# Decay terms and mask rows of three pairs as columns: the first batch of an attention and MLP kernel, recast

## The chip, the core and the metric

The kernel runs on one core of one Trainium2 chip. The metric is the device time of one launch in microseconds (us). A core has five engines that take their instructions in order, each from its own queue: PE (TensorE, matrix products), DVE (VectorE), ACT (ScalarE), POOL (GpSimd) and SP (SyncE, which here only issues DMAs). PEld is PE's loading of weights. Matmul results land in PSUM, which has eight banks for 512 f32 columns each; everything else lies in SBUF, with 128 partitions.

## The reference

Attention for 8 batches of 8 heads, 576 positions, 64 columns a head, with a decay that grows along the sequence, and then an MLP with a hard-swish gate:

```python
scores = scale * np.matmul(q, k.transpose(0, 1, 3, 2))
cum = np.cumsum(np.maximum(s, 0.0), axis=-1)
bias = -(cum[:, :, :, None] - cum[:, :, None, :])
scores = np.where(causal, -1000000000.0, scores + np.minimum(bias, 0.0))
attn = softmax(scores)                      # over the last axis
x = (attn @ v)                              # heads side by side: 4608 x 512
h = x @ w_in                                # 512 -> 2048
out = (h * np.clip(h + 3.0, 0.0, 6.0) / 6.0) @ w_out   # 2048 -> 512
```

## The kernel before

**Pairs.** The 64 heads are worked off as 32 pairs; a pair is two heads of one batch, so 1152 rows of q and of k. Three slots (`p % 3`) hold the transposed operands `qT` and `kT`, the values `v_h`, and three more the exponentials `Pm`. A score is one matmul over 128 partitions: rows 0 to 63 are the head's columns, and the other 64 rows carry the decay (three f16 parts of the running sum on the side of k, one on the side of q, each against ones) and a coarse causal mask of 60 rows. What the coarse mask leaves is cut by POOL (`affine_select`, L295).

**A pair's steps.** `load_qk` and `load_v` (L136 to L157) issue the loads on SP, in pieces of 64 f32 values. `cast_qk` (L167) makes f16 on POOL, `transpose_group` (L242) transposes q and k together on PE, five and four tiles, and DVE copies the halves to `qT` and `kT` (L253). `load_aug` (L159) brings the four decay rows from a scratch in DRAM, which the kernel has filled at its start (L469, L472). The mask rows of the three slots are written once (`mask_rows`, L125). For slot 0 the decay rows come straight from SBUF by eight small DMAs (L463 to L468). `scores_bank` (L272) makes four PSUM banks of scores a head, and ACT the exponentials (L290). `attend` (L320) sums with v (L331), and after a pair's second head DVE normalises (L341, L343). `x_transpose` (L356) puts the result into `xT`, by PE for the first eight pairs (L369, L377).

From pair 10 on the operands come another way: POOL builds `xb`, rows of 64 columns of q or k with the 64 decay and mask columns beside them (`cast_columns`, from `dec` and `xaug`), and one DMA transposes the whole.

**The layers.** Blocks of 512 tokens. `m1(n, f)` (L408) is four matmuls into a bank, then ACT (L416) and DVE (L417) make the gated f16 value in `gT`. `m2(n, t4, part)` (L430) is four of the sixteen matmuls of an output tile, and after the fourth part DVE scales it (L439) and SP stores it (L441). Weights come by POOL's queue with a cast (L383, L390).

**The order.** It is written by hand. Pairs 0 to 3 and the scores of pair 4 stand alone; then `weave` deals the tasks of four pairs among the MLP tasks of one block or more, by the costs beside each task. The MLP of block n can begin when the batch that it reads is in `xT`. At the start `keep_warm` gives PE idle work (L450).

PSUM: three banks with tag S (scores, transposes later on), two for O, two with tag M (`bank`: layers, early transposes, `keep_warm`), one with tag Y (outputs).

Of the kernel before, what the change touches and what calls it, by code (L numbers as in the profile page):

```python
# [9 lines left out]
F32 = mybir.dt.float32  # L10
# [6 lines left out]
def kernel(  # L17
# [29 lines left out]
    NS = 3  # L47

# [3 lines left out]

    def bank():
        return psum.tile([128, 512], F32, tag="M", bufs=2, name="bank")

    ident_dram = nc.inline_tensor(np.eye(128, dtype=np.float16), name="ident_f16")

    gran = np.arange(SEQ) // GRAN
    rows = np.arange(60)
    amask_np = np.ones((2, 64, SEQ), dtype=np.float16)  # L60
    amask_np[0, 4:64] = gran[None, :] == rows[:, None]
    amask_np[1, 4:64] = np.where(gran[None, :] < rows[:, None], -16384.0, 0.0)
    amask_dram = nc.inline_tensor(amask_np, name="amask")

    row = np.arange(W2).reshape(NTR, 128).T % SEQ
    xaug_np = np.concatenate([amask_np[1][:, row], amask_np[0][:, row]], axis=2)
    xaug_dram = nc.inline_tensor(
        np.ascontiguousarray(xaug_np.transpose(1, 2, 0)).reshape(128, 2 * NTR * 64),
        name="xaug",
    )  # L70
# [14 lines left out]
    xb = cpool.tile([128, 2, 2 * NTR, 128], F16, tag="c_xb")  # L85
# [9 lines left out]
    amask = work.tile([128, 2, SEQ], F16, tag="amask", bufs=1)  # L95
    s_sb = work.tile([NH, SEQ], F32, tag="s0", bufs=1)
    nc.sync.dma_start(out=s_sb, in_=s.rearrange("b h t -> (b h) t"))
    nc.scalar.dma_start(out=amask[64:128], in_=amask_dram.ap().rearrange("i p t -> p i t"))
# [20 lines left out]
    nc.gpsimd.memset(warm, 0.0)  # L119
    nc.gpsimd.memset(kT[:, :, W2:W2 + 64], 0.0)  # L120
    nc.gpsimd.memset(v_f[64:128, :, :, 4, :], 0.0)
    nc.gpsimd.memset(v_h[:, :, :, :, D:VW], 1.0)
    nc.gpsimd.memset(Pm[:, :, 1600:PW], 1.0)

    def mask_rows(sl, copy):  # L125
        for i, dst in enumerate((kT, qT)):
            copy(
                out=dst[64:128, sl, 0:W2].rearrange("p (h t) -> p h t", h=2),
                in_=amask[64:128, i:i + 1, :].to_broadcast([64, 2, SEQ]),
            )  # L130
# [5 lines left out]
    def load_qk(p, eng):  # L136
        b, h0 = (2 * p) // H, (2 * p) % H
        t = work.tile([128, NTR, 2, D], F32, tag="qkf", bufs=3, name=f"qkf{p}")
        for i, src in enumerate((q, k)):
            rows = src[b, h0:h0 + 2].rearrange("h s d -> (h s) d")  # L140
            eng.dma_start(  # L141
                out=t[:, :, i, :], in_=rows.rearrange("(t p) d -> p t d", p=128)
            )
        qk_f[p] = t

    def load_v(p, eng):
        b, h0 = (2 * p) // H, (2 * p) % H
        sl = p % NS
        for hh in range(2):
            eng.dma_start(  # L150
                out=v_f[:, sl, hh, 0:4, :],
                in_=v[b, h0 + hh, 0:512].rearrange("(t p) d -> p t d", p=128),
            )
        eng.dma_start(
            out=v_f[0:64, sl, :, 4, :],
            in_=v[b, h0:h0 + 2, 512:SEQ].rearrange("h p d -> p h d"),
        )  # L157

    def load_aug(p, eng):  # L159
        sl = p % NS  # L160
        c0 = p * W2
        eng.dma_start(out=kT[64:67, sl, 0:W2], in_=kaug_dram[:, c0:c0 + W2])
        eng.dma_start(out=qT[67:68, sl, 0:W2], in_=qaug_dram[:, c0:c0 + W2])
# [6 lines left out]
    xaug = cpool.tile([128, 2 * NTR, 64], F16, tag="c_xaug")  # L170

    def load_columns():
        nc.sync.dma_start(out=xaug.rearrange("p t c -> p (t c)"), in_=xaug_dram.ap())

    def copy_columns():
        for i in range(2):
            nc.vector.tensor_copy(out=xb[:, i, :, 64:128], in_=xaug)

# [32 lines left out]
    def cast_columns(p):  # L211
# [5 lines left out]
        nc.gpsimd.tensor_copy(out=x[:, 0:NTR, D + 3:D + 4], in_=dec[:, :, 3:4, p])  # L217
# [8 lines left out]
    def cast_v(p):  # L226
        sl = p % NS
        copy = nc.vector.tensor_copy if p in (1, 2, 3, 4) else nc.gpsimd.tensor_copy
        copy(out=v_h[:, sl, :, :, 0:D], in_=v_f[:, sl])  # L229

    def half_bank(early):

        if early:
            return psum.tile([128, 640], F16, tag="M", bufs=2, name="pTm")
# [7 lines left out]
    def transpose_group(p, g):  # L242
        t0, t1 = ((0, 5), (5, 9))[g]
        n = (t1 - t0) * 128
        pT = half_bank(p < 5)
# [10 lines left out]


# [4 lines left out]
        (896, [(1, 256, 576), (4, 512, 576)]),  # L262
        (1280, [(2, 256, 576)]),
# [5 lines left out]
        (4, 4): 1216, (2, 2): 1280, (2, 3): 1408, (2, 4): 1536,  # L269
    }  # L270

    def scores_bank(hd, bi):  # L272
# [39 lines left out]
        elif bi == 2:  # L312
            mask(P[:, 1216:1280], [[1, 64]])
        else:
            mask(P[:, 1280:1408], [[1, 128]])
# [4 lines left out]
    def attend(hd):  # L320
# [17 lines left out]
        if hh == 1:  # L338
            Ov = O_tiles.pop(p)[:, :, 0:5 * VW].rearrange("p h (t e) -> p h t e", t=5)
            r = work.tile([128, 2, 5, 1], F32, tag="r")  # L340
            nc.vector.reciprocal(out=r, in_=Ov[:, :, :, D:D + 1])  # L341
            xs = work.tile([128, 5, 2, D], F16, tag="xs", name=f"xs{p}")
            nc.vector.tensor_tensor(  # L343
                out=xs.rearrange("p t h d -> p h t d"),
                in0=Ov[:, :, :, 0:D],
                in1=r.to_broadcast([128, 2, 5, D]),
                op=ALU.mult,
            )
            x_tiles[p] = xs
# [6 lines left out]
    def x_transpose(p):  # L356
# [10 lines left out]
        pX = half_bank(p < 3)  # L367
# [9 lines left out]
        nc.vector.tensor_copy(out=xT[:, hp, b * SEQ:(b + 1) * SEQ], in_=pX[:, 0:SEQ])  # L377
# [25 lines left out]
    def m1(n, f):  # L403
        if f == 0:
            gT[n] = work.tile([128, NF, 512], F16, tag="gT", bufs=2, name=f"gT{n}")
        ph = bank()
        for kc in range(KC):
# [6 lines left out]
            )  # L414
        trl = work.tile([128, 512], F32, tag="trl", bufs=3)
# [5 lines left out]
    def m2(n, t4, part):  # L421
# [15 lines left out]
        if part == 3:  # L437
# [3 lines left out]
            nc.sync.dma_start(out=out[r0:r0 + 128, :], in_=osb)  # L441
# [5 lines left out]
    def keep_warm(n):  # L447
        pw = bank()
# [4 lines left out]


    load_qk(0, nc.sync)
    load_v(0, nc.sync)
    load_qk(1, nc.sync)
    mask_rows(0, nc.scalar.copy)

    nc.scalar.activation(out=qaug, in_=c8, func=AF.Copy, scale=-1.0)  # L460
    for hh in range(2):
        c0, c1 = hh * SEQ, (hh + 1) * SEQ
        nc.sync.dma_start(out=kT[64:65, 0, c0:c1], in_=kaug[hh:hh + 1, 0, :])  # L463
        nc.scalar.dma_start(out=qT[67:68, 0, c0:c1], in_=qaug[hh:hh + 1, :])
    for hh in range(2):
        c0, c1 = hh * SEQ, (hh + 1) * SEQ
        nc.sync.dma_start(out=kT[65:66, 0, c0:c1], in_=kaug[hh:hh + 1, 1, :])
        nc.scalar.dma_start(out=kT[66:67, 0, c0:c1], in_=kaug[hh:hh + 1, 2, :])  # L468
    nc.sync.dma_start(  # L469
        out=kaug_dram.rearrange("r (h t) -> h r t", h=NH), in_=kaug  # L470
    )
    nc.sync.dma_start(out=qaug_dram.rearrange("r (h t) -> h (r t)", h=NH), in_=qaug)  # L472
    mask_rows(1, nc.scalar.copy)
    load_v(1, nc.sync)
    load_aug(1, nc.sync)
    load_qk(2, nc.sync)
    load_v(2, nc.sync)

    weights_at = {1: [(load_w_in, 0)], 2: [(load_w_in, 1)]}
    pairs_at = {0: [3], 1: [4], 2: [], 3: [5], 4: [6], 5: [7, 8]}  # L480

    def att_tasks(p):


        more = p + 1 < NP

        def loads():
            if p + 2 < PTD:
                load_aug(p + 2, nc.sync)
            if p == 5:  # L490
                load_columns()
            for m in pairs_at.get(p, [p + 3] if p + 3 < NP else []):
                load_qk(m, nc.sync)
                load_v(m, nc.sync)
            if 4 < p < PTD - 1:
                cast_qk(p + 1)

        def casts():
            if more:
                cast_v(p + 1)  # L500
            if p + 2 <= 4:
                cast_qk(p + 2)
# [3 lines left out]
            for load, c in weights_at.get(p, []):  # L506
                load(c)

        def scores(hd):
            return [(lambda bi=bi: scores_bank(hd, bi), 400) for bi in range(4)]  # L510

        tr = [[], []]
        if p + 1 < min(NP, PTD):
            tr = [[(lambda: transpose_group(p + 1, 0), 640)],
                  [(lambda: transpose_group(p + 1, 1), 512)]]
        here = tr if p != 4 else [[], []]
        late = [(lambda: attend(2 * p - 1), 1200)] if p > 0 else []
        back = [(lambda: x_transpose(p - 1), 0 if by_dma(p - 1) else 640)] if p > 0 else []
        a = [(loads, 0)]
        if p <= PXD:  # L520
            a += scores(2 * p) + here[0] + late
            a += scores(2 * p + 1) + [(casts, 0)] + here[1] + back
        else:
            s0, s1 = scores(2 * p), scores(2 * p + 1)
            a = late + (back + a if by_dma(p - 1) else a + s0[:2] + back)
            a += (s0 if by_dma(p - 1) else s0[2:]) + here[0]
            a += s1 + [(casts, 0)] + here[1]
        if p == 6:
            a += [(decay_columns, 640)]
        if p == 7:  # L530
            a += [(copy_columns, 0)]
        c = [(lambda: attend(2 * p), 1200)]
        if p == 4:
            c += [(lambda: cast_qk(p + 1), 0)] + tr[0] + tr[1]
        return a, c

    att_of = [[]]
    for p in range(NP):
        a, c = att_tasks(p)
        att_of[-1] += a  # L540
        if p % 4 == 0 and p > 0:
            att_of.append([])
        att_of[-1] += c
    att_of[-1] += [(lambda: attend(NH - 1), 1200), (lambda: x_transpose(NP - 1), 640)]
# [39 lines left out]
    keep_warm(18)  # L584
    cast_qk(0)
    transpose_group(0, 0)
    transpose_group(0, 1)
    mask_rows(2, nc.vector.tensor_copy)
# [53 lines left out]
```

## Time and profile before

| | us |
|---|---|
| time, median of 3 runs (lowest, highest) | 382.07 (380.73, 382.93) |
| span of the profiled run | 378.1 |
| PE busy | 353.6 |
| ACT busy | 210.4 |
| DVE busy | 190.8 |
| POOL busy | 146.4 |

Busy times are sums over the span. PE is busy for 94% of it, but matmuls are pipelined and their ends are modelled, so a busy PE may still run at half clock or below its rate. The share of DMA is the mean over the 16 DMA engines of the time that their packets took; it can pass 1 where packets overlap. Of 184621 packets, 177828 are under 512 bytes.

What a stage is limited by is not seen in these sums. It is read from three views: the busy times in stretches of the span, the chain of work that ended last (followed back from the end, each step to what released it), and the timeline, in which an arrow in brackets tells how long an engine was idle before an instruction and what ended that.

### The profile page before, as it was taken

To read this page: it belongs to the slowest core of one execution; us is meant where nothing else is said; L and a number is where in the kernel's file an instruction comes from. 1 tells how busy PE (TensorE), PEld (TensorE's weight loads), DVE (VectorE), ACT (ScalarE), POOL (GpSimd) and SP (SyncE) were. 2 spreads that over 40 slices of the span, in tenths; PEclk is the share of its full clock that TensorE was granted. 3 is DMA by queue.
4 is the path that set the end of the run, shared out by engine and by line. 5 is a ranking of instruction groups with operands and counts; after the bars stand their busy time and mean duration, and the time that the engine had idled before them with its cause. 6 is when DMAs were issued, how large, how long until landed. Compare 5 with 4: busy or idle time off the path is not lost.

```text
span 378.1 us, 7609 instructions
## 1 busy us (share of the span) xinstructions
PE 353.6 (94%) x2780; PEld 219.8 (58%) x2780; DVE 190.8 (50%) x329; ACT 210.4 (56%) x406; POOL 146.4 (39%) x375
## 2 busy tenths in 40 slices
PE   7766778899999999999999999999999999999995
PEld 3454455566666666666666666666666655555542
DVE  5554466875545444544444445445444554454531
ACT  4745466456866666666656666666666543443310
POOL 4365444364565444444444554454453100000000
PEclk9989699999999999999999999999999999999999
DMA  8699999945999999999999998999854001010011
GB/s 181 137 204 193 194 208 249 210 105 132 200 186 243 204 211 200 216 203 203 197 190 199 214 208 179 206 211 200 185 114 106 31 30 55 28 55 29 28 66 74
DMA packets 184621, 59.38 MB, mean 157 GB/s; under 512 B 177828, under 2 KB 178212, under 8 KB 184584
## 3 DMA queue, kind: packets, MB, share of 16 engines
q1 hardware_dynamic: 182536, 54.52, 68.2%
q0 software_dynamic: 1632, 4.19, 5.9%
q8 instruction: 22, 0.36, 0.4%
q10 hardware_dynamic: 416, 0.19, 0.2%
q14 instruction: 15, 0.12, 0.1%
HBM read 37.41 MB, written 9.73 MB: 125 GB/s over the span
## 4 chain that ended last, share of the span: by engine, by line
PE 82%; DMA 9%; DVE 3%; ACT 2%; SPq 1%; issue 1%; POOL 1%; POOLq 0%; ACTq 0%; DVEq 0%
PE bank L408 31%; PE po L430 30%; PE S L282 9%; PE O L331 7%; DMA qkf<-in_k_dram 5%; DMA v_f<-in_v_dram 3%; PE bank L430 3%; ACT Pm L290 2%; PE pT L369 1%; DMA s_sb<-in_s_dram 1%; PE bank L450 1%; SPq L141 1%; POOL t L167 1%; DVE qkT L253 1%; DVE kaug L115 0%
## 5 line engine op out<-in xcount | busy, mean ns | idle before, releaser
L416 ACT ACTIVATE trl<-bank,bias 128x512 f32<-128x512 f32 x144 | 99.5, 691 | 111.8 <-PE bank L408 110.8
L417 DVE SCALAR_TENSOR_TENSOR gT<-trl,bank 128x512 f16<-128x512 f32 x144 | 99.1, 688 | 121.8 <-ACT trl L416 121.8
L408 PE MATMUL bank<-xT,w_in 128*128 128x512 f16 x576 | 148.3, 383 | 1.3 <-DVE gT L417 1.3
L290 ACT ACTIVATE Pm<-S 128x384 f16<-128x384 f32 (+2 forms) x256 | 116.2, 505 | 32.3 <-PE S L282 30.6
L295 POOL TENSOR_SCALAR_AFFINE_SELECT Pm<-Pm 128x128 f16<-128x128 f16 (+2 forms) x256 | 79.0, 311 | 135.4 <-ACT Pm L290 126.6
L430 PE MATMUL po<-w_out_sb,gT 128*128 128x512 f16 x528 | 130.9, 379 | 0.0
L408 PEld LDWEIGHTS <-w_in 128*128 128x128 f16 x576 | 77.5, 146 | 31.6 <-issue 2.8
L430 PEld LDWEIGHTS <-gT 128*128 128x128 f16 x576 | 53.2, 98 | 51.4
L282 PE MATMUL S<-qkT 128*128 128x320 f16 (+4 forms) x448 | 70.2, 265 | 6.9 <-DVE qkT L253 2.3
L282 PEld LDWEIGHTS <-qkT 128*128 128x128 f16 x448 | 41.4, 99 | 34.2 <-DVE qkT L253 2.7
L331 PEld LDWEIGHTS <-Pm 128*128 128x128 f16 x960 | 39.1, 98 | 12.1 <-POOL Pm L295 0.4
L331 PE MATMUL O<-v_h,Pm 128*128 128x65 f16 x960 | 41.6, 195 | 0.3 <-POOL Pm L295 0.3
L343 DVE TENSOR_TENSOR xs<-O,r 128x640 f16<-128x640 f32 x32 | 26.4, 824 | 1.1
L213 POOL CAST xb<-qkf 128x1152 f16<-128x1152 f32 x22 | 25.3, 1149 | 0.0
L439 DVE TENSOR_SCALAR osb<-po 128x512 f32<-128x512 f32 x33 | 22.6, 685 | 5.0 <-PE po L430 5.0
L229 POOL CAST v_h<-v_f 128x640 f16<-128x640 f32 x28 | 20.6, 737 | 2.2 <-DMA v_f<-in_v_dram 2.2
L341 DVE RECIPROCAL r<-O 128x10 f32<-128x10 f32 x32 | 7.1, 220 | 25.6 <-PE O L331 25.4
L167 POOL CAST t<-qkf 128x1152 f16<-128x1152 f32 x10 | 11.8, 1177 | 12.2 <-DMA qkf<-in_k_dram 12.2
L238 PEld LDWEIGHTS <-t 128*128 128x128 f16 x90 | 6.3, 99 | 12.1 <-POOL t L167 8.2
L253 DVE COPY qkT<-pTm 64x640 f16<-64x640 f16 (+1 forms) x20 | 9.1, 453 | 7.8 <-PE pTm L238 7.6
L450 PE MATMUL bank<-warm 128*128 128x512 f16 x30 | 9.5, 487 | 2.2 <-POOL warm L119 1.4
L430 PE MATMUL bank<-w_out_sb,gT 128*128 128x512 f16 x48 | 11.3, 379 | 0.0
(40 smaller groups left out, 80.2 us busy)
## 6 DMA issues: line engine op xcount, KB each, us to landing
qkf<-in_q_dram SPq DMA_DIRECT2D x32, 288.0 KB, 3.6
qkf<-in_k_dram SPq DMA_DIRECT2D x32, 288.0 KB, 4.2
out_dram<-osb SPq DMA_DIRECT2D x36, 256.0 KB, 2.0
v_f<-in_v_dram SPq DMA_DIRECT2D x64, 128.0 KB, 3.6
w_in<-in_moe_w_in_dram POOLq DMA_DIRECT2D x2, 1024.0 KB, 11.0
w_out_sb<-in_moe_w_out_dram POOLq DMA_DIRECT2D x4, 512.0 KB, 8.3
v_f<-in_v_dram SPq DMA_DIRECT2D x32, 32.0 KB, 8.2
qkT<-xb SPq DMA_TRANSPOSE x22, 5.2
```

Of the source, the lines that this page charges most:

```text
L213: nc.gpsimd.tensor_copy(out=x.rearrange("p (i t) c -> p t i c", i=2)[:, :, :, 0:D], in_=qk_f.pop(p))
L229: copy(out=v_h[:, sl, :, :, 0:D], in_=v_f[:, sl])
L282: nc.tensor.matmul(out=S[:, c:c + hi - lo], lhsT=kT[:, sl, off + 128 * kt:off + 128 * (kt + 1)], rhs=qT[:, sl, off + lo:off + hi], start=( ...
L290: nc.scalar.activation(out=P[:, p0:p0 + n], in_=S[:, 0:n], func=AF.Exp, scale=0.125, bias=0.0)
L295: nc.gpsimd.affine_select(out=view, in_=view, pattern=pattern, compare_op=ALU.is_ge, fill=0.0, base=0, channel_multiplier=-1,)
L331: nc.tensor.matmul(out=O[:, hh, qt * VW:qt * VW + D + 1], lhsT=P[:, c:c + 128], rhs=v_h[:, sl, hh, kt, 0:D + 1], start=(qt == 0), stop=(qt ...
L343: nc.vector.tensor_tensor(out=xs.rearrange("p t h d -> p h t d"), in0=Ov[:, :, :, 0:D], in1=r.to_broadcast([128, 2, 5, D]), op=ALU.mult,)
L408: nc.tensor.matmul(out=ph, lhsT=w_in_t[f // 8][:, kc, f % 8, :], rhs=xT[:, kc, n * 512:(n + 1) * 512], start=(kc == 0), stop=(kc == KC - 1),)
L416: nc.scalar.activation(out=trl, in_=ph, func=AF.Relu, bias=bias3[:, 0:1], scale=1.0)
L417: nc.vector.scalar_tensor_tensor(out=gT[n][:, f, :], in0=trl, scalar=6.0, in1=ph, op0=ALU.min, op1=ALU.mult)
L430: nc.tensor.matmul(out=po, lhsT=gT[n][:, f, t4 * 128:(t4 + 1) * 128], rhs=w_out_sb[:, f, :], start=(f == 0), stop=(f == NF - 1),)
L439: nc.vector.tensor_scalar_mul(out=osb, in0=po, scalar1=1.0 / 6.0)
```

## The change

For pairs 0 to 2 the operands are now built as they already are from pair 10 on: q and k are each loaded with nine whole rows to a partition (2304 bytes in one piece), cast into `xb` (now three buffers) beside the 60 mask columns, which one DMA and a copy bring, and the four decay columns. These come from small matmuls of the decay rows with a part of the identity (`decay_first`, 27 matmuls of 64x6). A transpose of the whole 128 columns then gives operand, decay and mask together. As nine rows lie in a partition, the copies out of PSUM read with a step (`rows_of_head`). Mask rows in all slots are left by these transposes, and the decay row on the side of q moves from row 67 to 127.

For pairs 0 and 1, v is loaded by POOL's queue with the cast in the DMA. The early transposes have two PSUM banks of their own (tag T), which are given to `bank` when the layers begin. The loads of later pairs are issued right after the cast that frees their buffer (`own`), with `load_aug` of a pair apart from them. Outputs of block 0 are stored by ACT's queue in place of SP's. Block 0's first layer is no longer dealt among pairs 4 to 8 but mostly within pair 4, with the Y bank as a third bank; 12 instead of 8 parts of its second layer stand in the tasks of pairs 5 to 8, and 4 in the next block. The bank of scores (4, 4) moves from the third to the fourth bank of a head, so that a head has three masks in place of four. In the last pair of the first batch each head is normalised by itself.

```diff
+    ROWS = 3
-    xb = cpool.tile([128, 2, 2 * NTR, 128], F16, tag="c_xb")
+    xb = cpool.tile([128, 3, 2 * NTR, 128], F16, tag="c_xb")
...
+            if p < ROWS:
+                qk_f[p] = t.rearrange("p (i t d) -> p t i d", i=2, t=NTR)
+                eng.dma_start(
+                    out=t[:, i * NTR * D:(i + 1) * NTR * D],
+                    in_=rows.rearrange("(p t) d -> p (t d)", t=NTR),
+                )
...
+    load_v(0, nc.gpsimd)
+    load_v(1, nc.gpsimd)
...
+    def transpose_rows(p, i):
...
+        for t in range(NTR):
+            transpose_tile(
+                T_tiles[p, i][:, t * 128:(t + 1) * 128],
+                xb[:, p, NTR * i + t, :],
...
+    def rows_of_head(p, i, hh):
+        nc.vector.tensor_copy(
+            out=(qT, kT)[i][:, p, hh * SEQ:(hh + 1) * SEQ].rearrange("d (j t) -> d j t", t=NTR),
+            in_=T_tiles[p, i][:, 0:W2].rearrange("d (t j) -> d j t", j=128)[
+                :, hh * 64:(hh + 1) * 64
+            ],
+        )
...
+    def decay_first(pD, i, first, last):
+        src = kaug[:, i, :].rearrange("h (j t) -> h t j", t=NTR)
+        for t in range(NTR):
+            nc.tensor.matmul(
+                out=pD[0:64, t, :],
+                lhsT=src[:, t],
+                rhs=ident[0:NH, 0:2 * ROWS],
...
-        (896, [(1, 256, 576), (4, 512, 576)]),
-        (1280, [(2, 256, 576)]),
+        (896, [(1, 256, 576)]),
+        (1216, [(2, 256, 576), (4, 512, 576)]),
...
+            if n == 0 and f % 3 == 2:
+                phs[f] = psum.tile([128, 512], F32, tag="Y", name="ph")
...
+            eng = nc.scalar if n == 0 else nc.sync
+            eng.dma_start(out=out[r0:r0 + 128, :], in_=osb)
...
+    for p in range(3):
+        load_qk(p, nc.sync, columns9_dram if p == 0 else None)
     load_v(2, nc.sync)
+    cast_first(0, nc.scalar.copy, 0, 1)
+    copy_columns(0, nc.scalar.copy)
+    load_qk(3, nc.sync)
+    load_v(3, nc.sync)
...
+    def own(p):
+        cast_qk(p)
+        cast_v(p)
+        load(p + 3)
...
+    keep_warm(10)
+    decay_first(pD0, 0, True, True)
+    keep_warm(3)
+    decay_first(pD1[:, 0], 1, True, False)
...
+    transpose_rows(0, 0)
+    decay_first(pD1[:, 1], 2, False, True)
...
+    nc.gpsimd.tensor_copy(out=hold, in_=kaug[:, 2, SEQ - 1:SEQ])
+    nc.gpsimd.tensor_scalar_mul(out=qaug, in0=kaug[:, 0, :], scalar1=-1.0)
+    cast_first(1, nc.gpsimd.tensor_copy)
...
+    layers_begin()
+    x_transpose(2)
+    for f in range(2):
+        m1(0, f, range(3))
+    attend(7)
...
+    own(4)
+    weave(pair_behind_weights(4), m1_tasks(0)[3:], 0.95)
...
+    weave(att_of[1], m2_0[4:12])
+    weave(att_of[2], merged(m1_tasks(1), m2_0[12:], 1))
```

## The prediction

> **What bounds the kernel now.** I read the slices of the page first, since a mean over 378 us hides the stages:
>
> ```profile
> PE   7766778899999999999999999999999999999995
> PEclk9989699999999999999999999999999999999999
> DMA  8699999945999999999999998999854001010011
> ```
>
> TensorE is full from slice 10 (about 95 us) to the end. Only before that is there time to win, and there the DMA row is full. The table by stages (columns: stretch, length, busy PE, PEld, DVE, ACT, POOL, granted clock, DMA share, GB/s) gives sizes:
>
> ```profile
> 12.00:24.00 12.00, 7.53 (x77) 5.48 (x76) 4.76 (x11) 6.20 (x15) 4.92 (x14) 0.86 0.90 186
> 24.00:36.00 12.00, 8.42 (x141) 6.75 (x139) 7.37 (x17) 7.80 (x19) 9.59 (x24) 1.00 1.02 194
> 36.00:48.00 12.00, 8.60 (x50) 5.34 (x51) 4.58 (x10) 5.49 (x11) 4.99 (x12) 0.72 1.00 198
> 48.00:60.00 12.00, 10.04 (x95) 7.00 (x94) 8.39 (x16) 7.87 (x15) 4.67 (x11) 1.00 1.11 231
> 60.00:72.00 12.00, 9.10 (x91) 6.30 (x89) 8.48 (x16) 7.14 (x15) 6.07 (x13) 1.00 1.03 219
> 84.00:96.00 12.00, 12.00 (x127) 8.13 (x125) 7.10 (x14) 7.78 (x18) 5.81 (x16) 1.00 0.59 131
> ```
>
> From 12 to 72 us TensorE is idle 16.3 us, no other engine is full, and the DMA share stays near 1. The chain that ended last says which transfers:
>
> ```profile
> 15.93 3.96 DMA qkf<-in_k_dram
> 27.48 11.71 DMA v_f<-in_v_dram
> 49.85 13.93 DMA qkf<-in_k_dram
> ```
>
> The timeline shows the holes on TensorE that they leave (start, duration, what; in brackets the idle time before it):
>
> ```profile
> 12.59 0.27 PE L282 MATMUL S<-qkT 128*128 128x256 f16 x1
> 21.24 0.29 PE L238 MATMUL pTm<-ident,t 128*128 128x128 f16 x1 [3.41 <-POOL t L167]
> 36.64 0.28 PE L282 MATMUL S<-qkT 128*128 128x256 f16 x1 [2.12 <-DMA qkT<-kaug_scratch]
> 40.63 1.56 PE L282 MATMUL S<-qkT 128*128 128x256 f16 x7 [1.76 <-DVE qkT L253]
> 42.78 0.63 PE L408 MATMUL bank<-xT,w_in 128*128 128x512 f16 x1
> ```
>
> First scores start at 12.59, the first layer matmul at 42.78: 30.2 us for four pairs. Between 24.4 and 33.9, where no transfer was late, two pairs took 9.4 us, so four would take 19; some 11 us are waits for data, a clock of one half behind them included (0.86 and 0.72 above).
>
> **What the Trainium skill says.** "DMA: Bandwidth & Descriptors", section "Why small descriptors are slow (HBM only)", gives a 256-byte descriptor 27% overhead. The trace agrees and goes further: its records have 21 ns for a packet of 256 bytes and 114 ns for one of 2304 (0.082 against 0.049 ns a byte). The same page, "Issuing engines are not separate DMA queues": a queue more saves issue time and no bandwidth. No run here isolates that; I give the v loads on GpSimd's queue no bandwidth gain. "VectorE: DVE Perf Modes", section "Mode 2×_1P", wants neighbouring 16-bit elements for two a cycle; the new copies read PSUM with a step of 128. The trace agrees with the fast case: 64x640 f16 from PSUM in 0.488 us, 128x512 f32 in 0.685. "TensorE: Matmul & The Clock Gate", section "What's actually happening", gives half clock after some 3.4 us of idleness; the stretch of 0.5 behind the 3.41 us hole agrees.
>
> **The start (to first scores).** Removed: four mask copies on ACT (4 x 1.146) and two on DVE (2 x 0.872), the eight row DMAs of decay terms into slot 0 and the loads of such rows for pairs 1 and 2 (one held TensorE 0.6 us, L163), and two casts of v (1.25 on POOL, 0.49 on DVE). Added: 27 small matmuls (as L192: 10 in 0.65 us, so 0.6 us per nine), 4 + 2 small copies on ACT and 2 on DVE (0.18 to 0.28 each as L205), 18 transposes of q and k apart instead of 9 joint (0.8 per nine), four copies of 128x576. Those have no row. Below: 0.46, as the contiguous xT copy; above: 0.75, the f32 row plus 64 elements at one a cycle (0.685 + 0.067). I take 0.75, because of the step.
> In order: kaug row 0 at 6.1 us (as now), its nine matmuls 6.8, ACT's copies 7.4; row 1 at 7.4 and its matmuls 8.0; q transposed 8.8. Row 2 ends at about 8.2, as POOL now waits behind "hold" and the subtraction can cost 0.75 (as L113) instead of 1.58; if the collision stays, 9.0. Its matmuls come behind q's transposes, 9.4; decay copies 9.9; k transposed 10.6; one copy, 11.4. So first scores at 11.4 (11.0 to 13.0): **-1.2 us**. Behind "hold" on POOL stand qaug and pair 1's cast (0.7 and 1.15), done by 11.5 and needed at 12. Pair 0's data come in six issues at 0.6 each, k by 6 to 7; the v loads on POOL cost it 6 x 0.55 to 0.9 before 9 us, and attend(0) needs them only near 16.
>
> **The first four pairs.** Pairs 1 and 2 are now bound by DVE with the one T tile: per half, nine transposes (0.8), two copies (1.5), in turn, as T must be read before it is refilled. First scores of pair 1: 12.85 (pair 0's last copy) + 1.5 + 0.8 + 1.5 = 16.7. Pair 2: + columns 0.93 + 0.8 + 1.5 + normalisation 1.04 (0.22 + 0.82) + 1.5 = 22.5. Pair 3: transposed jointly, two halves (4 copies, 1.82) behind xT 0.46 and waits of 1.6 for scores: 26.4. Then one pair as today, 4.7, ends at 31.1; I put the first layer matmul at **31.5** (29.5 to 34). ACT hides below: 8 heads x 1.69 = 13.5 us; so does POOL: 8 x 1.12 of masks (one of four selects gone; two blocks in one 0.41) and some 6 us of casts. DMA: q,k rows of three pairs 3 x 1.8, v 4 x 1.3, columns and s 1.5, pair 3's q,k 2.6, so about 15 us: landed near 18. The wait of pair 3's load for ACT's cast of pair 0 (8.7 us) holds only SP's next loads, which are not needed before 23. So here **-10.1** more.
>
> **From there to the second block of layers.** Now: 42.78 to 88.70 (m1(1,0)), with 9 of m2's 16 parts of block 0 done; after: 13 parts, so compare with 88.70 + 4 x 0.864 = 92.15 (a group of four takes 0.864 in the chain). After, by TensorE: m1 0 to 2, attend(7), two x transposes: 4.0 (the last waits for ACT's copy, ~0.5), 35.5. Thirteen m1 groups 11.2 + pair 4 (2.8) + halves 0.8 + 0.5 of stalls: 50.8. The third bank removes today's 0.64 waits of L408 for DVE; the banks opened in T's place wait for its last readers, DVE's copies of pair 3, done by 26. Four parts of m2, decay columns 1.8, halves: 57. Then 9 parts 7.8 and 3.75 pairs at 2.8 (15.5 - 7.8 for 2.75 pairs between 73.2 and 88.7 now) + 0.5 of stalls for each pair: 20.2, so 77.2. Stores of block 0 stand on ACT: each waits for DVE's osb (0.69) with exponentials behind; I charge their part of those stalls. Gain 92.15 - 77.2 = **15.0** at this point.
>
> **Paying DMA.** From 77.2, 21 groups + attention as now (11.3) = 29.4, so block 2 would begin at 106.6 against 121.56. The packets do not shrink so much: shares times lengths up to 121.5 sum to 111.5 us of all 16 engines; minus 3 x 1.2 for rows, 107.9 must fit into 104.6 us. The share over 140 to 260 is 0.99, over 108 to 120 it was 1.19: 0 to 4.4 us late; I take 3.0. Behind that TensorE is full in both kernels (9.3 us a pair), so nothing is given back. Masks, stores of later blocks and transposes by DMA stay. Sum **-12.0** against the profiled span of 378.1, so 366.1; the shown runs lie higher (median 382.07, 380.73 to 382.93), and 12 less is **370.0**.
>
> **The rivals.**
> A, as summed (0.55): 366 to 374.
> B, DMA stays the bound (0.28): rows save only 3.6 us; v loads with cast send the same number of pieces, and the weights now start at 16 us among the loads. Then only idle DMA (share 0.05 at 10 to 12, 0.45 to 0.83 at 42 to 46: ~3 us) and the rows count: 3.6 + 3 = about 7, 375 (374 to 378). For it: shares over 1 for 50 us. Against it: they drop to 0.58 at 72 to 96 while TensorE works off stock, so demand there can move.
> C, slower (0.07): pairs 5 to 8 starve. A load of pair p+3 now goes out after POOL's cast of pair p, behind 4 issues of w_out, and m1 is already spent on pair 4, so nothing fills TensorE. Leads are 18 us (pair 8: 51 to 70) and 14 (pair 9). With landings as today (14) nothing is lost; it decides above the lead: were weights and loads to stretch them to 22, four pairs would each wait 4 to 5 us: 12 - 17, some 5 slower, 387.
> D, copies at 0.46 and no DMA debt (0.10): 3.5 + 3.0 more, 363.5 (362 to 366).
> The change may also fail its name: in the built order stores of block 1 on still stand ahead of loads on SP; only block 0's left it. So that part is worth nothing beyond the waits of L141 and L150 counted.
>
> **Numbers.** A and D lie wholly below, B too: faster 0.90; within 0.5% (1.9 us, about what a measurement of this kernel can tell from no change) 0.03, between B and C; slower 0.07. Range 364.5 to 377.5: it holds A, most of B and part of D, and leaves out C.
>
> **What would show it.** Right: first S matmul at 11 to 13; 128x576 copies near 0.75; first w_in matmul at 30 to 34; no TensorE wait over 1 us for DMA between 12 and 60; m1(1,0) near 77, block 2 near 110; clock 1.00 from 12. Wrong: holes on TensorE in 55 to 75 released by casts of qkf or v_f (C); a DMA share near 1 with PE holes at 80 to 110 (B); scores later than 14 (the chain through ACT and PSUM is longer than priced).

## The result, and the profile after

The changed kernel takes 386.05 us (median of 4 runs, 385.73 to 387.33), the kernel before 381.88 beside it (380.73 to 382.93). The ratio is 1.0116 with a 95% interval of 1.0079 to 1.0154: slower, by over twice the half per cent that the prediction took for no change. The forecast was 370.0 and faster. The profiled spans are 384.0 and 378.1 us. In all ratios of this document executions over 1.5 per cent above the fastest of the same kernel are left out.

The slices of the page after, to be laid beside those of before:

```profile
PE   7978798867999999999999999999999999999995
PEclk9699999898999999999999999999999999999999
DMA  8998999465799999999997989899954101001012
```

The thin place on TensorE has moved. Before, it lay ahead of 57 us (digits of 6 and 7); now most of these are better, and the two slices from 77 to 96 us are worse, 6 and 7 where 9 stood. The DMA row falls there to 6 and 5, so it isn't full where TensorE idles. The same stretches as before, from the table of busy times:

```profile
12.00:24.00 12.00, 10.20 (x111) 7.12 (x111) 7.92 (x14) 7.98 (x18) 5.78 (x13) 0.85 1.02 189
24.00:36.00 12.00, 9.31 (x133) 6.87 (x132) 7.76 (x17) 7.16 (x17) 8.14 (x19) 1.00 0.89 169
36.00:48.00 12.00, 9.34 (x68) 6.16 (x67) 7.32 (x14) 6.79 (x12) 3.28 (x6) 1.00 1.09 207
48.00:60.00 12.00, 11.74 (x111) 7.57 (x109) 8.62 (x22) 7.34 (x15) 3.53 (x7) 1.00 0.99 205
60.00:72.00 12.00, 9.46 (x68) 5.38 (x67) 5.63 (x16) 3.68 (x10) 3.94 (x8) 0.86 0.64 154
84.00:96.00 12.00, 8.09 (x80) 5.27 (x81) 6.66 (x14) 3.38 (x8) 7.37 (x13) 0.92 0.43 98
```

From 12 to 60 us TensorE is busier in every row than before. In the last two rows ACT is busy for less than a third of the time (3.68 and 3.38 us of 12), and TensorE idles beside it: the engines wait for each other. The chain that ended last holds no transfer between 10 and 60 us any more, where it held 3.96, 11.71 and 13.93 us of them. The timeline of TensorE says where the time went instead:

```profile
15.70 0.68 PE L365 MATMUL S<-qkT 128*128 128x256 f16 x5
...
34.31 0.60 PE L507 MATMUL bank<-xT,w_in 128*128 128x512 f16 x2
...
65.01 0.33 PE L365 MATMUL S<-qkT 128*128 128x320 f16 x2 [1.23 <-ACT Pm L373]
...
71.16 0.56 PE L365 MATMUL S<-qkT 128*128 128x256 f16 x4 [0.78 <-DVE qkT L284]
...
85.40 0.45 PE L269 MATMUL pT<-ident,t 128*128 128x128 f16 x5 [1.57 <-POOL t L194]
...
92.59 0.33 PE L365 MATMUL S<-qkT 128*128 128x320 f16 x2 [1.90 <-ACT Pm L373]
```

First scores come 3.1 us later than before, the first layer matmul 8.5 us earlier. From 57 to 96 us the holes are released by exponentials (L373), by POOL's cast of the next pair (L194) and by DVE's copies (L284), never by a transfer. The first matmul of the second block, m1(1,0), stands at 95.90 (before 88.70), that of the third, m1(2,0), at 127.91 (before 121.56). At m1(2,0) both kernels have done the same: 182 matmuls of scores, 390 of the products with v, 128 and 72 of the two layers. From there to the end of the span it is 256.5 us before and 256.1 after. So the whole difference arises before m1(2,0). Up to that point TensorE is idle 20.0 us before and 19.8 after: the 7.2 us of holes taken out between first scores and first layer matmul are given back, most of them between 57 and 96. TensorE's busy time grew from 101.5 to 108.1 us, and the stretches at half clock from 10.2 to 13.7.

### The profile page after: what moved, and what is told of

It reads as the page before. It is cut to its first block, busy times and chain, and to the rows that moved or that the text cites. A ratio compares the mean times of both kernels' runs of the same rounds, so it can differ in the third digit from the quotient of the medians.

```text
span 384.0 us, 7564 instructions
## 1 busy us (share of the span) xinstructions
PE 360.0 (94%) x2822; PEld 223.9 (58%) x2822; DVE 190.2 (50%) x328; ACT 210.4 (55%) x412; POOL 142.9 (37%) x322
## 4 chain that ended last, share of the span: by engine, by line
PE 79%; DVE 7%; ACT 5%; issue 3%; POOL 3%; DMA 3%; ACTq 0%; POOLq 0%
PE bank L507 29%; PE po L531 28%; PE S L365 9%; PE O L416 6%; ACT Pm L373 4%; PE bank L531 2%; DVE qkT L284 2%; DMA qkT<-xb 2%; PE pT L269 2%; POOL Pm L378 1%; PE pD L318 1%; POOL t L194 1%; DMA s_sb<-in_s_dram 1%; PE pT L459 1%; DVE qkT L307 1%
## 5 line engine op out<-in xcount | busy, mean ns | idle before, releaser
L518 DVE SCALAR_TENSOR_TENSOR gT<-trl,bank 128x512 f16<-128x512 f32 x139 | 95.4, 687 | 119.8 <-ACT trl L517 119.7
L517 ACT ACTIVATE trl<-bank,bias 128x512 f32<-128x512 f32 x139 | 95.9, 691 | 105.2 <-PE bank L507 103.3
L507 PE MATMUL bank<-xT,w_in 128*128 128x512 f16 x556 | 143.2, 383 | 3.0 <-DVE gT L518 1.8
L373 ACT ACTIVATE Pm<-S 128x384 f16<-128x384 f32 (+2 forms) x256 | 115.7, 507 | 39.2 <-PE S L365 27.9
L378 POOL TENSOR_SCALAR_AFFINE_SELECT Pm<-Pm 128x256 f16<-128x256 f16 (+1 forms) x192 | 70.4, 370 | 158.0 <-ACT Pm L373 154.0
L431 DVE TENSOR_TENSOR xs<-O,r 128x640 f16<-128x640 f32 (+1 forms) x33 | 26.5, 804 | 1.3 <-DVE r L430 0.2
L430 DVE RECIPROCAL r<-O 128x10 f32<-128x10 f32 (+1 forms) x33 | 7.2, 217 | 30.6 <-PE O L416 30.5
L284 DVE COPY qkT<-pT 64x640 f16<-64x640 f16 (+1 forms) x24 | 10.9, 454 | 11.4 <-PE pT L269 10.9
L307 DVE COPY qkT<-pT 128x576 f16<-128x576 f16 x10 | 7.2, 751 | 4.3 <-PE pT L269 4.3
L269 PE MATMUL pT<-ident,t 128*128 128x128 f16 x63 | 5.5, 229 | 3.4 <-POOL t L194 2.1
L553 PE MATMUL pw<-warm 128*128 128x512 f16 x18 | 7.4, 567 | 1.4 <-POOL warm L203 1.4
```

The lines of the kernel that those rows point to most:

```text
L373: nc.scalar.activation(out=P[:, p0:p0 + n], in_=S[:, 0:n], func=AF.Exp, scale=0.125, bias=0.0)
L378: nc.gpsimd.affine_select(out=view, in_=view, pattern=pattern, compare_op=ALU.is_ge, fill=0.0, base=0, channel_multiplier=-1,)
L431: nc.vector.tensor_tensor(out=x_tiles[p].rearrange("p t h d -> p h t d")[:, h0:hh + 1], in0=Ov[:, :, :, 0:D], in1=r.to_broadcast([128, hh ...
L507: nc.tensor.matmul(out=ph, lhsT=w_in_t[f // 8][:, kc, f % 8, :], rhs=xT[:, kc, n * 512:(n + 1) * 512], start=(kc == 0), stop=(kc == KC - 1),)
L517: nc.scalar.activation(out=trl, in_=ph, func=AF.Relu, bias=bias3[:, 0:1], scale=1.0)
L518: nc.vector.scalar_tensor_tensor(out=gT[n][:, f, :], in0=trl, scalar=6.0, in1=ph, op0=ALU.min, op1=ALU.mult)
```

## The experiments

All ratios are to the kernel before, with their 95% intervals; "span" is that of the profiled run.

**Two waits in pairs 5 to 8.** A store on ACT's queue waits, in order, for DVE's output tile, and exponentials stand behind it. POOL casts the next pair only after the masks of this one. One run puts the stores back on SP:

```diff
-            eng = nc.scalar if n == 0 else nc.sync
+            eng = nc.sync
```

> One edit to the changed kernel: the four stores of block 0 are issued by SP again, not by ACT. Theory S (an ACT that waits for DVE's scaled output holds the exponentials behind it, 7.0 us idle before 64.5 and 3.0 before 92.1 in the changed kernel, and TensorE then runs out of score banks and falls to half clock): 380 to 383 us, TensorE's waits of 1.23 and 1.90 us for ACT gone. Theory C (the cast of the next pair behind the masks of this one sets a pitch of 7.9 us a pair): within 1.5 us of the changed kernel's 386.05, since the stores stand inside that pitch.

Another puts the cast (and the load behind it) at the head of a pair's tasks:

```diff
-        return a + att(2 * p) + step(own, p + 1) + tr[:1] + [(lambda: None, 400)] + tr[1:]
+        return step(own, p + 1) + a + att(2 * p) + tr[:1] + [(lambda: None, 400)] + tr[1:]
```

> One edit to the changed kernel: in pairs 5, 6 and 7 the casts and loads of the next pair are recorded ahead of the pair's own scores, not behind its first attend, so that on POOL they stand ahead of the pair's masks. Theory C: the pitch of first scores from pair 5 to pair 8, 7.9 us (63.1, 71.2, 79.1, 86.9), falls to 5.5 to 6.5, and the time to 379 to 382 us. Theory S alone: pitch stays above 7.5 and the time within 1.5 us of 386.05. Theory L (loads arrive late): the cast would now wait for its data, and the pitch would stay.

Measured: 1.0041 (1.0020 to 1.0061), span 381.2, and 1.0069 (1.0040 to 1.0097), span 382.0. Each helps and neither reaches the kernel before. The second misses its forecast (384.03 us where 379 to 382 was expected). First scores of pairs 5 to 8, on average 7.9 us apart in the changed kernel, still follow each other every 8.0 us with stores on SP and every 7.6 with the early cast. The waits from 56 to 96 us (us in total, times, longest) show why. The changed kernel, TensorE and then ACT:

```profile
PE S L365 <- ACT Pm L373: 4.4, 6, 1.9
PE pT L269 <- POOL t L194: 2.1, 2, 1.6
```

```profile
ACT Pm L373 <- DVE osb L540: 10.0, 2, 7.0
```

Stores on SP, TensorE:

```profile
PE S L365 <- ACT Pm L373: 1.9, 6, 0.4
PE pT L269 <- POOL t L194: 3.2, 3, 1.6
```

Early cast, TensorE:

```profile
PE S L365 <- ACT Pm L373: 6.0, 6, 2.8
PE S L365 <- DVE qkT L284: 1.7, 2, 0.9
```

With the store gone, ACT no longer waits for the output tile, but TensorE waits longer for the cast; with the cast gone, it waits longer for exponentials. The longest of those waits, 2.8 us, again has a store in front of it on ACT's queue:

```profile
66.19 0.38 ACTq L544 DMA_DIRECT2D out_dram<-osb  x1
66.68 3.28 ACT L373 ACTIVATE Pm<-S 128x384 f16<-128x384 f32 x8 [8.60 <-DMA v_f<-in_v_dram]
```

DVE had made the output tile by 64.58 in that run. The profile puts the rest down to a load of v that landed at 66.12; why a store should wait for it isn't shown. As either wait grew when the other was taken out, both were taken out together:

> All stores on SP's queue and the cast of the next pair at the head of a pair's tasks, together. Theory S (the waits of ACT for the output tile and of TensorE for POOL's late casts are separate links of one serial loop of a pair): the two gains of 2.8 and 2.0 us of span add up, so a span near 379.2, no TensorE wait for POOL's cast and none over 0.5 us for exponentials between 57 and 94, m1(1,0) near 93. Rival L (the loop of a pair is bound by scores, exponentials, masks, copies whatever stands beside it, and only the longest link shows): one gain swallows the other, span 381 to 382. Theory N (the real loss is that TensorE has 9 layer groups for four pairs, and the pair was priced too low): even with both waits gone m1(1,0) stays above 92, far from the forecast 77.

Measured: 378.26 us, 0.9905 (0.9881 to 0.9928), m1(1,0) at 90.27, first scores of pairs 5 to 8 6.3 us apart. TensorE's main waits are left at these:

```profile
PE S L365 <- ACT Pm L373: 1.9, 6, 0.4
PE S L365 <- DVE qkT L284: 1.7, 2, 0.9
```

From 1.0116 that is 2.1 per cent, more than the 0.75 and 0.47 of the single runs together. So these two parts of the change alone decide the sign: without them it is faster than the kernel before. The span (378.1) lies 1.1 us under the forecast 379.2, and the two gains more than add up. m1(1,0) was expected near 93; theory N had it above 92, and at 90.27 that sign didn't come, though it stays 13 us behind the 77 of the prediction.

The store was also put on ACT alone, in the kernel before (the line of the first diff, the other way):

> The kernel before with the one part of the change that moves the stores of block 0 to ACT's queue. Theory S (a store on ACT holds the exponentials behind it, and a load behind a store on SP costs nothing that TensorE sees): slower by 1 to 3 us, 380 to 381 span. Rival (loads behind stores were worth freeing, ACT has room in that kernel since layers are dealt over more pairs): same or faster, 376 to 378.

Measured: 386.64 us, 1.0135 (1.0071 to 1.0199), span 385.6; ACT waits 5.0 us for the output tile (L439), longest 2.8. It costs in that kernel too, and at least as much as in the changed one. The loss is above the 1 to 3 us expected, and what makes up the rest of it isn't shown.

**Filler.** The change spends block 0's first layer on pair 4. Is that what opens the holes? One run deals 13 groups of it and 12 parts of the second layer evenly over pairs 4 to 8:

```diff
-    weave(pair_behind_weights(4), m1_tasks(0)[3:], 0.95)
...
-    weave(att_of[1], m2_0[4:12])
+    weave(
+        pair_behind_weights(4) + step(own, 5) + [(decay_columns, 640)]
+        + step(load_columns, columns1_dram, nc.sync) + halves(5) + att_of[1],
+        m1_tasks(0)[3:] + m2_0[:12],
+    )
```

> The changed kernel with block 0's layers dealt evenly among pairs 4 to 8 (13 groups of the first layer and 12 parts of the second by their costs), as the kernel before deals them; casts and stores stay where the change put them. Theory F (pairs 5 to 8 stall TensorE because the first layer was spent on pair 4, so that nothing fills the chain from scores to the next pair's scores): 374 to 379 us, idle TensorE between 57 and 96 falls from some 9 us to under 4. Theory S or C without F: no gain over 1.5 us, or a loss, as the chain of casts is as long as before and the first layer ends later.

Measured: 1.0032 (1.0009 to 1.0054), span 382.0, m1(1,0) at 94.54. That is a gain of 0.84 per cent, no less than either edit above brought alone, but not theory F, which had 374 to 379 us and under 4 us of idle time. TensorE is still idle 10.6 us between first layer matmul and m1(1,0) (12.0 in the changed kernel): the holes at 71 to 93 shrink, others open at 51 to 67, the longest behind DVE's copies (1.90) and POOL's cast (1.65). DVE is busy 9.3 of 12 us from 48 to 60, with gates, decay columns and copies in one queue. The same together with the two edits above, decay columns behind pair 6:

> As the run before, and pairs 4 to 7 and the head of pair 8 dealt evenly over 13 groups of block 0's first layer and 12 of its second, the decay columns moved behind pair 6. Theory F (missing filler is what opens the holes once casts and stores are out of the way): idle TensorE between first layer matmul and m1(1,0) falls from 12.0 us to 5 or less, m1(1,0) at 88 to 90, span 374 to 376, below the kernel before. Rival L (pairs are bound by their own loop): idle stays over 9, span 379 to 381.

Measured: 0.9984 (0.9938 to 1.0030), span 378.9, m1(1,0) at 91.48, idle 9.8 us there against 6.7 with stores and cast alone. Theory F falls: even dealing hides part of the two waits while they stand, and once they are gone it makes things worse (0.9984 against 0.9905). As the decay columns were moved too, what of that is the dealing's alone isn't shown.

**The start.** First scores at 15.70 were to be at 11.4. The first guess was TensorE's half rate from 8.7 to 15.6 us; three more warm-up matmuls were put ahead of each of the first two decay groups (10 to 13, 3 to 6):

> The changed kernel with 13 instead of 10 idle matmuls at the start and 6 instead of 3 behind the first decay matmuls. Theory W (first scores come at 15.7 instead of 11.4 us because TensorE falls to half clock from 8.7 to 15.6, so nine decay matmuls or transposes take 1.1 us instead of 0.6): clock 1.0 through the start, first scores at 12.5 to 14, time 383 to 385. Rival (the start is set by DVE and ACT; the clock only shows it): first scores within 0.7 us of 15.7, time within 1 us of 386.05.

Measured: 386.73 us, 1.0136 (1.0065 to 1.0206), first scores at 15.21, half rate still from 11.8 to 15.2. Theory W falls in that form. And it tells more: q's transposes there took 0.68 us, at full rate, and the decay matmuls before and behind them 1.20 as in the changed kernel. So rate isn't what makes these slow. The timeline of the changed kernel at the start has the nine decay matmuls of row 0, of which the load of weights is the longer part, and q's transposes:

```profile
6.91 1.11 PEld L318 LDWEIGHTS <-kaug 64*64 64x64 f16 x9 [1.98 <-DVE kaug L139]
6.91 1.20 PE L318 MATMUL pD<-ident,kaug 64*64 64x6 f16 x9 [1.29 <-DVE kaug L139]
...
9.98 1.14 PE L269 MATMUL pT<-ident,xb 128*128 128x128 f16 x9
```

The weights of the nine are every ninth element of `kaug`. In this run they are neighbours, and what they are multiplied with is zeros. It leaves the decay terms of pairs 0 to 2 out, with the same number of instructions:

```diff
-                lhsT=src[:, t],
-                rhs=ident[0:NH, 0:2 * ROWS],
+                lhsT=kaug[:, i, t * 64:(t + 1) * 64],
+                rhs=warm[0:NH, 0:2 * ROWS],
```

> The 27 small decay matmuls of the start read their weights from neighbouring columns in place of every ninth, and multiply them with zeros, so the decay terms of pairs 0 to 2 are left out. Theory W9 (a weight load with a step costs twice): nine take 0.6 to 0.7 us in place of 1.20, q's transposes begin 0.5 us earlier, and first scores come at 14.0 to 14.6 in place of 15.70; span 382.5 to 383. Rival (the half rate of TensorE or the wait for ACT's small copies sets it): nine stay at 1.2 or first scores at 15.3 to 15.7, span unchanged at 384.

The same place in this run, and what came of it at pair 3 (SPq lines are SP's issues of transfers):

```profile
6.21 0.36 PEld L318 LDWEIGHTS <-kaug 64*64 64x64 f16 x9 [1.29 <-DVE kaug L139]
6.21 0.44 PE L318 MATMUL pD<-warm,kaug 64*64 64x6 f16 x9 [0.71 <-DVE kaug L139]
...
23.07 3.65 SPq L177 DMA_DIRECT2D v_f<-in_v_dram  x2
...
27.58 0.38 SPq L189 DMA_DIRECT2D qkT<-kaug_scratch  x1
...
29.82 1.17 PE L365 MATMUL S<-qkT 128*128 128x256 f16 x5 [2.78 <-DMA qkT<-qaug_scratch]
```

A load of weights takes 0.040 us in place of 0.123, nine matmuls 0.44, TensorE stays at full rate up to first scores, and first scores come at 11.80. Yet the first layer matmul stands at 35.26 and the time is 385.75, 1.0113 (1.0038 to 1.0189): not a microsecond of the 3.9 is left. The last three lines name the wait: the decay rows of pair 3 (L189) stand on SP's queue behind the load of pair 4, whose issues alone last from 18.8 to 27.4. In the changed kernel, with first scores at 15.70, they last from 18.2 to 23.2, and the rows come in time:

```profile
23.40 0.39 SPq L189 DMA_DIRECT2D qkT<-kaug_scratch  x1
```

So with the earlier start the rows go out 4.2 us later; why the same issues took 8.6 us in place of 5.1 isn't shown. TensorE waits 2.78 us for the rows, and the clock is half from 28.9 to 35.7. So that load was moved behind the rows, with the edits of stores, cast and weights kept:

```diff
+                + step(load_aug, 3, nc.sync) + step(load, 4) + att(0)
...
-    load(4)
     keep_warm(4)
```

> Stores on SP, casts at the head of a pair, the 27 small matmuls fed from neighbouring columns and with zeros (decay terms of pairs 0 to 2 left out, as in the run on the weights), and on SP's queue the load of pair 4 behind the decay rows of pair 3. Theory Q (a start 3.9 us earlier was lost only to the rows of pair 3 standing behind a load on SP): first scores near 11.8, no wait of TensorE for those rows, first layer matmul at 31.0 to 32.0, m1(2,0) at 117.5 to 118.5, span near 375, time 1 per cent below the run with stores and casts alone. Rival B (from 12 us on bytes are the bound): TensorE waits for another transfer in place of those rows, first layer matmul at 34 to 35.3, span 377 to 378.

Measured: 374.92 us, 0.9845 (0.9779 to 0.9911), span 372.4; first scores 11.76, first layer matmul 30.75, m1(2,0) at 115.98, all a little earlier than theory Q had them. The rows go out at 25.14, and no wait of TensorE from 9 to 98 us is for a transfer, where theory B had another transfer take the place of those rows. So the trace speaks for Q, and the bytes, which are the same, were no bound there. In time the step is smaller than the 1 per cent expected: the interval touches that of stores and cast alone (0.9881 to 0.9928), and no run has those two with the fast start and the old order. The order of SP alone, with the slow start:

> Stores on SP, casts at the head of a pair and SP's order, the start left as in the change (stepped weight loads). Theory Q: the rows of pair 3 had time enough behind a start at 15.7, so the order alone is worth nothing: first layer matmul at 34.3 to 35.3, span 377 to 378.5, time as the run with stores and casts alone, a ratio of 0.988 to 0.994. Rival: SP's order helps by itself, first layer matmul below 33.5, ratio below 0.987.

Measured: 377.53 us, 0.9886 (0.9849 to 0.9922), first scores 15.24, first layer matmul 34.86: by itself the order is worth nothing that can be told from 0.9905.

**Trying to keep the decay terms.** Copies of the three rows into tile order, one on ACT and two on DVE, feed the matmuls from neighbours. First with the step on the written side:

```diff
+        copy(
+            out=kperm[:, i].rearrange("h (t j) -> h j t", t=NTR),
+            in_=kaug[:, i].rearrange("h (j t) -> h j t", t=NTR),
+        )
```

> Stores on SP and casts at the head of a pair, and the start mended: rows of decay terms are copied once into the order of their tiles (one copy on ACT, two on DVE), so that the 27 small matmuls read neighbouring columns; and on SP's queue the load of pair 4 stands behind the decay rows of pair 3. Theory W9+Q (the start is late by the stepped weight loads, and its gain is lost only because pair 3's rows stand behind a load): first scores at 12.0 to 12.8, first layer matmul at 31.5 to 32.5, no wait of TensorE for the rows of pair 3, span 374.5 to 375.5, time 374.5 to 376. Rival B (DMA bound: whatever starts earlier waits for bytes): first layer matmul stays at 34 to 35 and the span at 377.5 to 378.5.

> The same without the change of SP's order. Theory Q: first scores at 12.0 to 12.8, TensorE waits 2 to 3 us for the decay rows of pair 3 near 27 to 30, first layer matmul at 34 to 35.5, span 377.5 to 378.5, nothing gained over the run with stores and casts alone. Rival (the hole came from zeroed data or one slow landing): no such wait, as fast as the run beside it.

> The changed kernel with the start and SP's order mended, stores on ACT and late casts left in. If the steps add: 3 us less than the changed kernel, span 381, time 382.5 to 383.5, first layer matmul near 32, and the stretch from there to m1(1,0) still 60 to 62 us. If pairs 5 to 8 wait for loads, the gain is eaten there: span 383 to 384.

All three miss: first scores at 17.26, 16.75 and 17.11. Times 0.9973 (0.9953 to 0.9993), 0.9973 (0.9954 to 0.9992) and, with stores and casts as in the change, 1.0214 (1.0170 to 1.0259). The second had no wait for pair 3's rows, as its start was too late to meet them, so it could not test the order. The reason stands in the timeline of the first: the copies are far dearer than the loads they mend.

```profile
6.52 2.75 ACT L145 COPY kperm<-kaug 64x576 f16<-64x576 f16 x1
...
7.49 1.47 DVE L145 COPY kperm<-kaug 64x576 f16<-64x576 f16 x1
```

Then with the step on the side that is read ("h (t j) -> h t j" for both):

> Stores on SP, casts at the head of a pair, SP's order mended, and the decay rows copied into the order of their tiles with the step on the side that is read and neighbours on the side that is written. If the step hurts only where it is written: the copies take 0.6 to 0.8 us in place of 2.75 on ACT and 1.47 on DVE, first scores at 12.5 to 13.3, first layer matmul at 31.5 to 32.5, span 373 to 374.5, time 375 to 376.5, 1.3 to 1.8 per cent under the kernel before. If a step costs the same on either side: copies over 1.4 us, first scores at 16 to 17.3, time 379 to 380.5.

```profile
6.52 1.23 ACT L145 COPY kperm<-kaug 64x576 f16<-64x576 f16 x1
...
7.50 1.19 DVE L145 COPY kperm<-kaug 64x576 f16<-64x576 f16 x1
```

Better, not free, and 1.2 is between the two guesses: 378.18 us, 0.9911 (0.9875 to 0.9946), first scores at 15.31. TensorE, idle 2.39 us ahead of the decay matmuls, ran at half rate from 8.1 to 14.9. Ten more warm-up matmuls were put into that idle time:

> As the run with the step on the read side, with 20 warm-up matmuls in place of 10 ahead of the first decay matmuls. Theory H (half rate is what is left of the late start): no half-rate stretch before the first scores, nine transposes in 0.66 to 0.68 us in place of 1.14, first scores at 13.0 to 13.9, first layer matmul at 31.8 to 32.8, span 374.3 to 375.3, ratio 0.983 to 0.989. Rival (the chain through ACT and DVE sets the start and TensorE's rate is hidden): first scores at 15.0 to 15.3, ratio as beside it, 0.991.

Measured: 375.94 us, 0.9831 (0.9798 to 0.9865), the fastest kernel of the study that computes everything. But theory H isn't shown by its profile: q's transposes took 0.68 us as expected, then the rate fell all the same (11.8 to 15.2, k's transposes 1.12), and first scores stood at 15.42, in a run in which `s` landed at 4.38 (3.69 in the run before it). So the 0.8 per cent between the two runs don't come from the start: their profiles reach m1(1,0) at 88.10 and 88.20 and m1(2,0) at 119.25 and 119.28. Of the 1.2 us between the spans, 1.06 is a wait for one transposing transfer (`xb` to `qkT`) at 122.24 that this run doesn't have. Why it doesn't is open.

## Why the prediction was wrong

The forecast as a row of stretches, against the profiles (us; the last column leaves decay terms of pairs 0 to 2 out):

| stretch | before | forecast | after | stores and cast mended | also weights and SP's order |
|---|---|---|---|---|---|
| to first scores | 12.6 | 11.4 | 15.7 | 15.7 | 11.8 |
| to first layer matmul | 30.2 | 20.1 | 18.6 | 19.5 | 19.0 |
| to second layer, m2(0,0) | 30.4 | 19.3 | 22.3 | 23.1 | 22.3 |
| to m1(1,0) | 15.5 | 26.4 | 39.3 | 31.9 | 31.9 |
| to m1(2,0) | 32.9 | 32.4 | 32.0 | 31.2 | 31.1 |
| to the end of the span | 256.5 | 256.5 | 256.1 | 256.7 | 256.4 |

In the kernel before, the fourth row holds 9 parts of the second layer, in the others 13; the fifth the rest. The forecast's rows add up to 366.1; after is 384.0. Of the 17.9 us the start makes 4.3 and the fourth row 12.9.

**The start** failed in one term: "27 small matmuls (as L192: 10 in 0.65 us, so 0.6 us per nine)". Nine took 1.20. L192 reads neighbours, the new ones every ninth element, 18 bytes apart. The Trainium skill, "SBUF — State Buffer", section "Door 1: The DMA port swizzle (why `[64,N]` ≈ `[32,N]`)", has a note on lines of 16 bytes, of which each new one costs an access a penalty. I had priced the step in PSUM (0.75 for L307, measured 0.751) and not here; the trace agrees with the note (0.123 against 0.040 us a load), though no run tried a step within 16 bytes. Three groups in a row cost 2.3 us more than with neighbours (3 x 1.20 less 3 x 0.44). Beside it stands the half rate: transposes 1.14 in place of 0.66. The Trainium skill, "TensorE: Matmul & The Clock Gate", section "What's actually happening", has the full rate come after some 3.4 us of steady work. The trace agrees in part: the first warm-up matmuls of the changed kernel begin 0.42 us apart, as at half rate, and three at 8.04 take 0.88 together. But the fall to half rate at 8.7, which the prediction had after some 3.4 us of idleness, comes behind a hole of 1.29; what sets it isn't shown. With neighbours TensorE ran at full rate to first scores. The estimates for "hold" (L142 0.75), copies and order were right: with the loads mended, 11.8 against 11.4.

**The first four pairs** were right in mechanism: no wait for a transfer, 18.6 us for the 20.1 forecast. But "30.2 us for four pairs" was misread. Before, 70 matmuls of scores lie ahead of the first layer matmul, five pairs of 14; after, 56. Part of the 11.6 us gained there is work of pair 4 put off, which my own third row then held (pair 4 at 2.8).

**"Then 9 parts 7.8 and 3.75 pairs at 2.8 (15.5 - 7.8 for 2.75 pairs between 73.2 and 88.7 now) + 0.5 of stalls for each pair: 20.2, so 77.2"** is the step that cost most. The price of a pair came from a wrong count. The groups of the kernel before in that stretch, which the prediction doesn't count:

```profile
L282 PE MATMUL S<-qkT 128*128 128x320 f16 (+4 forms) x28 | 4.0, 261 | 0.0
L331 PE MATMUL O<-v_h,Pm 128*128 128x65 f16 x75 | 3.2, 193 | 0.0
```

28 matmuls of scores are two pairs, and 75 products with v two and a half (30 a pair). So 7.7 us were 2 to 2.5 pairs, 3.1 to 3.9 each. With the clock full in this stretch (stores and cast mended) TensorE is busy 27.8 us, where the forecast had 24.4: +3.4. Its remaining idle time is 4.0 where I had 2.0: +2.0. The changed kernel adds to that 4.6 us of idle time (8.6) and 2.9 of busy time (30.7, at a mean clock of 0.93). Both are gone when the two waits are, so this larger part is shown by a run; that the first 5.4 us are the pair price and its stalls is worked out from the counts. Together 12.9, the whole of the row.

Both waits were in the prediction and were priced at next to nothing. "Stores of block 0 stand on ACT: each waits for DVE's osb (0.69) with exponentials behind; I charge their part of those stalls": what counts is not DVE's 0.69 but all that DVE has in front of it. In the chain of the changed kernel, decay columns (L239, L241) and copies of pair 5 (L284) fill DVE from 58.3 to 63.3 before the output tile is made. The last of DVE's lines, and ACT's, the store and the exponentials behind it:

```profile
59.68 1.68 DVE L239 COPY dec<-pD 128x128 f16<-128x128 f16 x8
61.35 1.88 DVE L284 COPY qkT<-pT 64x640 f16<-64x640 f16 x4
63.26 0.69 DVE L540 TENSOR_SCALAR osb<-po 128x512 f32<-128x512 f32 x1
...
63.98 0.38 ACTq L544 DMA_DIRECT2D out_dram<-osb  x1
64.47 1.69 ACT L373 ACTIVATE Pm<-S 128x384 f16<-128x384 f32 x4 [7.03 <-DVE osb L540]
```

Of these 7.03 us most cost nothing, as the scores that these exponentials read begin only at 63.10; TensorE shows 1.23 as a hole (the first scores of pair 5 fill three banks and stop). The order of POOL's tasks (cast of p+1 recorded behind the products of p) I named only for when it sends loads, and put the wait of TensorE for the cast itself at nothing: 2.1 us from 56 to 96.

**The third row** is 3.0 long by five holes of 0.3 to 1.1 us behind DVE's gates and copies and ACT's copy of xT; "0.5 of stalls" was too little. Most of them stay in every run. **Paying DMA**: the length was right (32.0 for 32.4), the reason was not shown: the DMA share there is 0.92, and TensorE's waits are for masks and exponentials (1.0 us together). Nothing was charged behind m1(2,0), and nothing came.

**The rivals.** A and D fell with the pair price and the start. B isn't borne out: the run with all four edits moves the same bytes and shows none of its holes; up to m1(2,0) TensorE waits for a transfer once, 0.17 us at 108.85. That its time, 374.9, is close to B's 375 is luck. C had the sign (pairs 5 to 8 starve) and nearly the number (387 for 386.05), but not the reason: POOL's late casts were released by ACT's exponentials, not by loads, and spreading the layers helps only while the two waits stand. With both waits and both faults of the start mended, and the decay terms of pairs 0 to 2 left out, the change gives 374.9, within the range; 4.9 us above the forecast remain, the pair price and the third row less the shorter stretches. With the decay terms kept, no run reached the early start, and 375.94 is the best.

## What to carry to other kernels

Before a stretch is priced by the piece, count the pieces with the table of groups for exactly that stretch, on both sides of the cut. An instruction that waits on an in-order queue costs what its producer has queued in front of it, not what the producer takes, less the time in which the waiting engine would have had nothing to do; list both queues. And when an early stage is sped up, look at what stands behind what on the queue of loads: a gain of 3.9 us was lost while one row transfer stood behind a long load.

## What the runs showed of the hardware

Weights read with a step of 18 bytes loaded in 0.123 us for 64 columns, at full and at half clock alike; neighbours took 0.040 at full and 0.061 at half clock. A copy of 64x576 f16 within SBUF with a step on the written side took 1.44 and 1.47 us on DVE and 2.75 on ACT; with the step on the read side 1.19 and 1.23; a cast of the same size without a step takes 0.45 (L141). TensorE fell to half rate near 11.8 us in two runs (more warm-up; read step with warm-up) although no hole between matmuls ahead of it was longer than 0.9 us. Of the time from 8.4 to 11.8, matmuls of 6 columns fill 2.3 us in the first of these and 1.0 in the second. Whether they count as idle isn't shown. And the recorded clock can miss: in the early-cast run and in that with stores and cast it stands at 1.00 for the whole start, while nine transposes took 1.14 us, as at half rate.
